# Spreading a kernel's weight loads over a phase of small products, and moving some vector work behind the results that free TensorE

## The chip, the cores and the metric

The kernel runs on one core of a Trainium2 chip. The metric is device time of one execution in microseconds; the values given are the median of several runs and the runs' own spread. The profile is one further execution, recorded by the hardware profiler. Its times count from the start of the profiled span.

## The reference

Two blocks follow each other. The first is a delta-rule attention with a state per head, the second a two-layer network with a PReLU between the layers.

```python
# q, k, v: (4, 8, 768, 48); beta: (4, 8, 768)
for t in range(S):
    y[:, :, t] = einsum('bhd,bhde->bhe', q[:, :, t], state)
    v_old = einsum('bhde,bhd->bhe', state, k_n[:, :, t])      # k_n: k by its norm
    state = state + beta_t * einsum('bhd,bhe->bhde', k_n[:, :, t], v[:, :, t] - v_old)
# x: y as (3072 tokens, 384); w_in: (384, 2048); w_out: (2048, 384)
h = x @ w_in
g = maximum(h, 0) + alpha * minimum(h, 0)
out = g @ w_out
```

The weights w_in and w_out arrive as float64, 6.3 MB each; everything else that matters here is float32.

## The kernel before, in words

The sequence of 768 tokens is cut into 12 chunks of 64, and the batch of 4 into 2 pairs. A step is one chunk of one pair with all its heads, so there are 24 steps. Within a step the recurrence over the 64 tokens is replaced by products of small matrices: the keys are transposed (`flip`, L383), their Gram matrix is made (`grams`, L435) and weighted, a triangular matrix is inverted, and the state is applied and renewed (`through_state` L774, `solve` L799, `outputs` L812, `next_state` L828). The triangular inverses of four steps at a time are made together. Its blocks of 32 are turned so that VectorE eliminates them column by column (`eliminate`: two instructions for each column, L527 and L533, between transposes, L500). For the first four steps only blocks of 16 are eliminated, and the halves are joined by small products on TensorE (`cross`, L604, L614 and L621, "the cross products").

The order on every engine is written out by hand. All instructions of an engine stay in program order, and `weave` mixes several generators by shares: each gives its pieces evenly over the length of the mixture, some starting at a given fraction of it. SP issues nearly all DMAs, in program order; each waits on SP for its buffer to be free, and what stands behind it waits too.

The loads of a step are `load_early` (keys, tile ke, 2 DMAs), `load_q` (qp, 2), `load_v` (v_raw, 2) and `load_late` (keys in another layout, kl, 4). Step n takes ke three steps ahead.

The weights are converted from float64 to float32 in the kernel. `weights` cuts a matrix into pieces, fetches each as raw 32-bit words into a staging place (L209), and converts it by two ScalarE instructions (`begin`, L225 and L226) and two VectorE instructions (`finish`, L235 and L240). w_in has 12 pieces of 512 KB. Their staging places are six parts of the w_out tile, which is not needed yet: pieces 0 to 5 are fetched at once, and each later piece when the one that had its place is converted. w_out has 16 pieces of 384 KB. Their places are three in a tile of their own, `space_out`, and four in the upper half of w_out.

The part that the change touches begins with `first_chunk`, which takes steps 0 and 1 through the attention. `second_pair` then does steps 2 and 3, mixed by `alongside` with the first layer of chunk 0 (`ffn_in(0)`, L942: eight pairs of 128 columns of w_in, in two banks by turns) and with the conversions. A bank of `ffn_in` is freed when ScalarE has made its negative part (L952) and VectorE the PReLU from it (L954). Two weaves follow: `ffn_in(1)` with conversions of w_out and 15 of the elimination's pieces (`SOON`), and `ffn_out(0)` (L985) with the remaining ones. Later, in the steps JOINED = 6 to 23, a step has three stretches; `PIECES_OF` gives the share of elimination pieces for each, and `weight_sums` (L929) makes differences of quarters of w_out for a faster form of the second layer.

Of the kernel before, what the change touches and what calls it, by code (L numbers as in the profile page):

```python
# [43 lines left out]
def kernel(  # L44
# [94 lines left out]
    def load_early(n, *queues):  # L139
        if n < N:  # L140
            fetch(k, n, early(n)[:, :, 0:D], *queues)
# [29 lines left out]
    SPACES = 3  # L171
# [7 lines left out]

    ahead = [0]  # L180

    def weights(pieces, stages, ids, done):

        count = len(pieces)
        fetched, begun = [], []

        def words(i):
            w = stages[ids[i]]
            dst, src = pieces[i]
            shape = list(dst.shape)
            n = shape[1] * (shape[2] if len(shape) > 2 else 1)
            w = w[:, 0 : 2 * n]  # L200
            if len(shape) > 2:
                return w.rearrange("p (f e) -> p f e", f=shape[1]), n
            return w, n

        def fetch(n):
            while len(fetched) < min(n, count):
                i = len(fetched)
                assert ids[i] not in ids[len(done) : i]
                nc.sync.dma_start(out=words(i)[0], in_=pieces[i][1].bitcast(U32))  # L209
                fetched.append(i)  # L210

        def flat(x):
            return x.rearrange("p f d -> p (f d)") if len(x.shape) > 2 else x

        def halves(i):
            w = flat(words(i)[0]).rearrange("p (e w) -> p e w", w=2)
            return w[:, :, 0], w[:, :, 1], flat(pieces[i][0])

        def begin(n):
            while len(begun) < min(n, count):  # L220
                i = len(begun)
                assert i < len(fetched)
                lo, hi, dst = halves(i)

                nc.scalar.activation(dst.bitcast(U32), lo, ACT.Copy, scale=2.0**-29)  # L225
                nc.scalar.activation(  # L226
                    lo.bitcast(FP32), hi.bitcast(FP32), ACT.Prelu, scale=2.0**-112, alpha=-(2.0**32)
                )
                begun.append(i)

        def finish():
            for i in range(count):
                begin(min(i + 2, max(ahead[0], i + 1)))
                lo, _, dst = halves(i)
                nc.vector.tensor_scalar(  # L235
                    out=lo, in0=lo, scalar1=3, scalar2=None, op0=ALU.logical_shift_left
                )
                yield

                nc.vector.tensor_tensor(  # L240
                    out=dst.bitcast(U32), in0=lo, in1=dst.bitcast(U32), op=ALU.add
                )
                done.append(i)
                n = len(fetched)
                while n < count and ids[n] not in ids[i + 1 : n]:
                    n += 1
                    fetch(n)
                yield

        return fetch, begin, finish()  # L250
# [94 lines left out]
    def squared(n):  # L345
        ksq[n] = work.tile([128, H, D], FP32, name="ksq", bufs=2)
        nc.scalar.square(ksq[n], early(n)[:, :, 0:D])  # L347

    def norms(n):
        stats[n] = work.tile([128, H], FP32, name="norm", bufs=EARLY + 3)  # L350
        nc.vector.tensor_reduce(out=stats[n], in_=ksq.pop(n), axis=AXX, op=ALU.add)  # L351
# [67 lines left out]
    def now(pieces):  # L419
        for x in pieces:  # L420
            x()
# [40 lines left out]
    NJ = 4  # L462
# [965 lines left out]
    def first_chunk(mask, convert):  # L1428

        both = (0, 1)  # L1430
        ahead[0] = n_in

        waits, pause = iter([0.5] * 2), []
        middle = cross(
            0, slice(0, 2 * H), edge, half_way, lambda: pause and busy(next(waits, 0), pause[0])
        )
        next(middle)
        pause.append(ps_one())
        busy(1, pause[0])
        begin_in(6)  # L1440
        for i in both:
            scale_v(i)
            mask(i)
        convert(2)
        next(middle)
        busy(1.25)
        place(0, (0,))
        place(1, (0,), True)
        for i in both:
            place(i, (1,), True)  # L1450
            now(between_1(i))
        keys = flipped(NJ, ps_ffn())
        convert(2)
        for i in both:
            place(i, (2,))
            now(between_2(i))
        now(keys)
        for i in both:
            now(through_state(i))
            now(solve(i))  # L1460
        now(flipped(NJ + 1, ps_ffn()))
        for i in both:
            now(outputs(i))
        convert(4)
        for i in both:
            to_ffn(i, ps_ffn())
        now(flipped(NJ + 2, ps_one()))
        for i in both:
            squared(NJ + i)
        load_early(NJ + NKE)  # L1470
        ahead[0] = FT * DM
        convert(4)
        for i in both:
            norms(NJ + i)

    def statics(first, last):
        if first > 0:
# [21 lines left out]
    ]  # L1499
    n = 2 * W_IN_P  # L1500
    n_in = FT * DM // n
    ids = [i % n_in for i in range(len(pieces))]
    fetch_in, begin_in, conv_in = weights(
        pieces, [space[:, i * n : (i + 1) * n] for i in range(n_in)], ids, in_done
    )
    PARTS_IN = 2 * len(pieces)

    pieces = [(w_out[:, f], moe_w_out[f * 128 : (f + 1) * 128]) for f in range(FT)]
# [19 lines left out]
    fetch_in(n_in)  # L1528
    squares(0)
    betas()  # L1530
    for _ in statics(0, NJ - 1):
        pass
    nc.scalar.copy(inside, ones)
# [22 lines left out]
            pass  # L1556

    first_chunk(mask, convert)
    fetch_out(SPACES)
    assert n + 22 == PARTS_IN + 10  # L1560

    first_in = ffn_in(0)
# [6 lines left out]
    def second_pair():  # L1569

        n, m, x = 2, 3, NJ
        both = (n, m)
        halves = [cross(0, slice(i * H, i * H + H), edge, half_way) for i in both]
        for i in range(2):
            now(next_state(i))
            load_late(i + 2)
            load_v(i + 3)
            alongside(2, 1)
        for h in halves:
            next(h)  # L1580
        flips(x + 3, n)
        load_early(x + 1 + NKE)
        load_q(n + 2)
        squares(x + 2)
        now(weigh(x))
        alongside(5, 2)
        next(halves[0])
        flips(N, m)
        load_early(x + 2 + NKE)
        load_q(n + 3)  # L1590
        now(weigh(x + 1))
        place(n, (0,))
        alongside(4, 2)
        next(halves[1])
        now(weigh(x + 2))
        place(m, (0,))
        alongside(2, 1)
        now(grams(x))
        squares(x + 3)
        alongside(2, 1)  # L1600
        for i in both:
            now(between_1(i))
        now(grams(x + 1))
        load_early(x + 3 + NKE)
        alongside(7, 3, (chain(*(placing(i, (1, 2, 3)) for i in both)), 6))
        for i in both:
            now(between_2(i))
        now(grams(x + 2))
        for i in both:
            scale_v(i)  # L1610
        now(weigh(x + 3))
        alongside(5, 3)
        y = ps_big()
        pieces = []
        for i in range(2):
            pieces += through_state(n + i, None, y[:, :, i * G * D : (i + 1) * G * D])
        now(pieces)
        alongside(5, 3)
        y = ps_big()
        pieces = []  # L1620
        for i in range(2):
            pieces += solve(n + i, y[:, :, i * G * D : (i + 1) * G * D])
        now(pieces)
        now(grams(x + 3))
        alongside(5, 2)
        y = ps_big()
        pieces = []
        for i in range(2):
            pieces += outputs(n + i, y[:, :, i * G * D : (i + 1) * G * D])
        now(pieces)  # L1630
        alongside(5, 2, (part(blocks, PIECES), PIECES))
        for i in both:
            to_ffn(i)
        for i in both:
            alongside(2 * (m - i), 0)
            now(next_state(i))
            load_late(i + 2)
            load_v(i + 3)
        alongside(IN_PARTS - 46, 1, (part(blocks, 1), 1))

    blocks, BEGUN, SOON, LAST = eliminate(1), PIECES + 1, 15, 6
    second_pair()
    fetch_out(len(stages))
    weave(
# [3 lines left out]
    for i in range(2):  # L1648
# [1 line left out]
    load_q(NJ + 2)  # L1650
    n = WHOLE + PIECES - BEGUN - SOON
    weave(
        (conv_out, OUT_PARTS // 2), (part(blocks, n), n),
        (statics(FIRST + NJ, EARLY + 3), 2 * (EARLY + 4 - FIRST - NJ) + 1),
        (ffn_out(0, True), OUT_PARTS),
    )
# [61 lines left out]
    for n in range(NJ, JOINED):  # L1718
# [7 lines left out]
    assert next(late, None) is None  # L1726
    PIECES_OF = {
        JOINED: (3, WHOLE - 2 * PIECES - 6 - 2 * share - 3, 2 * PIECES),
        JOINED + 1: (1, 4, 7), JOINED + 2: (4, 4, 5),
    }  # L1730
    TURNS = [(3, 3, 4), (3, 3, 4), (4, 4, 4), (0, 5, 6)]
    FILL = {JOINED: (8, 12, 12), JOINED + 1: (10, 12, 10), JOINED + 2: (8, 10, 12)}
# [2 lines left out]
    for n in range(JOINED, N):  # L1735
# [4 lines left out]
        if n == JOINED:  # L1740
            place(n + 1, (0,))
            extra[1] = [(weight_sums(1, 0, 3), 3)]
            extra[2] = [(weight_sums(0, 3, 4), 1)]
        elif n == JOINED + 1:
            extra[0] = [(weight_sums(1, 3, 4), 1), (placing(n + 1, (1, 2, 3)), PLACING)]

        later = burst_a(n)
        stretch(fill[0], blocks, share[0], later, *extra[0], *put_off)
# [63 lines left out]
```

## Time and profile before

| | |
|---|---|
| median of 3 runs | 664.44 us (662.76 to 664.89) |
| profiled execution | 665.1 us, of it the span 663.3 us |
| TensorE busy | 642.9 us, 97% of the span |
| VectorE busy | 491.9 us, 74% |
| ScalarE busy | 263.9 us, 40% |
| GpSimd busy | 92.9 us, 14% |
| moved by DMA | 37.72 MB in 110,963 packets |
| granted TensorE clock | 1.00 |

The profile names engines PE (TensorE), DVE (VectorE), ACT (ScalarE), POOL (GpSimd) and SP. PEld is the loading of weights into TensorE, which overlaps its products. A busy share is the mean over the whole span, and the stages differ: the transfers lie mostly in the first sixth, and VectorE is near its limit in some stretches and half idle in others. In a list of waits each row gives who waited, for whom, the total, how often, and the longest. In a timeline each row gives start and duration, the operation and its shapes, and in brackets the idle time before it with what ended it.

### The profile page before, as it was taken

To read this page: it belongs to the slowest core of one execution; us is meant where nothing else is said; L and a number is where in the kernel's file an instruction comes from. 1 tells how busy PE (TensorE), PEld (TensorE's weight loads), DVE (VectorE), ACT (ScalarE), POOL (GpSimd) and SP (SyncE) were. 2 spreads that over 40 slices of the span, in tenths; PEclk is the share of its full clock that TensorE was granted. 3 is DMA by queue.
4 is the path that set the end of the run, shared out by engine and by line. 5 is a ranking of instruction groups with operands and counts; after the bars stand their busy time and mean duration, and the time that the engine had idled before them with its cause. 6 is when DMAs were issued, how large, how long until landed. Compare 5 with 4: busy or idle time off the path is not lost.

```text
span 663.3 us, 22123 instructions
## 1 busy us (share of the span) xinstructions
PE 642.9 (97%) x9545; PEld 567.3 (86%) x9545; DVE 491.9 (74%) x1180; ACT 263.9 (40%) x621; POOL 92.9 (14%) x201
## 2 busy tenths in 40 slices
PE   5997999999999999999999999999999999999997
PEld 4576888556788988998998998988999999999997
DVE  4964799967999869748859748858868658568383
ACT  4945766334454252243343243232135245042140
POOL 6000210100000100001000000000035044053250
PEclk9999999999999999999999999999999999999999
DMA  8848645301432122122112111112111210100000
GB/s 119 249 119 223 157 108 141 84 25 35 73 67 49 26 53 46 26 49 50 26 38 37 27 38 37 26 38 38 26 41 35 41 32 4 31 9 2 24 1 25
DMA packets 110963, 37.72 MB, mean 57 GB/s; under 512 B 104161, under 2 KB 107249, under 8 KB 110865
## 3 DMA queue, kind: packets, MB, share of 16 engines
q1 hardware_dynamic: 109088, 35.81, 24.5%
q8 instruction: 75, 1.23, 0.7%
q10 hardware_dynamic: 1776, 0.49, 0.4%
q14 instruction: 24, 0.19, 0.1%
HBM read 31.56 MB, written 4.72 MB: 55 GB/s over the span
## 4 chain that ended last, share of the span: by engine, by line
PE 79%; DVE 12%; DMA 3%; ACT 3%; issue 1%; ACTq 0%; SPq 0%; DVEq 0%
PE p_ffn L1007 17%; PE p_ffn L942 16%; PE p_more L1259 8%; PE p_ffn L985 5%; PE p_more L1175 4%; PE p_ffn L1165 3%; PE p_ffn L1259 3%; PE p_ffn L1170 2%; PE p_pair L383 2%; PE p_pair L685 2%; DMA ke<-in_k_dram 2%; PE p_pair L774 2%; PE p_pair L799 2%; PE p_pair L1403 2%; PE p_pair L812 2%; PE p_pair L435 2%
## 5 line engine op out<-in xcount | busy, mean ns | idle before, releaser
L942 PE MATMUL p_ffn<-xt,w_in 128*128 128x256 f32 x768 | 176.1, 383 | 2.0 <-DVE act L954 2.0
L942 PEld LDWEIGHTS p_ffn<-xt,w_in 128*128 128x128 f32 x768 | 142.4, 190 | 22.6 <-issue 2.9
L954 DVE SCALAR_TENSOR_TENSOR act<-act,al_t,p_ffn 128x256 f32<-128x256 f32 x112 | 48.7, 476 | 29.1 <-ACT act L952 29.1
L952 ACT ACTIVATE act<-p_ffn 128x512 f32<-128x512 f32 x56 | 33.3, 595 | 82.4 <-PE p_ffn L942 82.2
L533 DVE TENSOR_TENSOR block<-block,prod 128x30 f32<-128x30 f32 (+9 forms) x150 | 49.9, 332 | 5.1
L1199 POOL TENSOR_TENSOR k_t<-k_t 128x128 f32<-128x128 f32 (+1 forms) x48 | 29.2, 609 | 167.4 <-ACT k_t L1194 164.9
L527 DVE TENSOR_TENSOR prod<-block 128x30 f32<-128x30 f32 (+9 forms) x150 | 48.8, 326 | 1.3
L1007 PE MATMUL p_ffn<-w_out,act 128*128 128x192 f32 x288 | 49.6, 328 | 0.0
L372 POOL TENSOR_TENSOR beta_t<-beta_t,rec 128x8 f32<-128x8 f32 x24 | 6.5, 270 | 291.7 <-DVE rec L370 275.2
L1007 PEld LDWEIGHTS p_ffn<-w_out,act 128*128 128x128 f32 x288 | 46.5, 190 | 0.3
L853 ACT COPY xt<-p_pair 128x384 f32<-128x384 f32 x22 | 10.4, 478 | 90.7 <-PE p_pair L851 76.9
L1199 POOL TENSOR_TENSOR block<-block 128x128 f32<-128x128 f32 (+1 forms) x48 | 27.6, 575 | 17.3 <-ACT block L1194 14.8
L1165 PE MATMUL p_ffn<-xt,w_in 128*128 128x256 f32 x96 | 28.7, 381 | 0.5 <-DVE o_sb L1027 0.5
L784 DVE TENSOR_TENSOR r<-v_raw,p_pair 64x192 f32<-64x192 f32 (+1 forms) x66 | 23.3, 353 | 2.3 <-PE p_pair L774 1.2
L351 DVE TENSOR_REDUCE norm<-ksq 128x8 f32<-128x384 f32 x24 | 12.9, 546 | 16.2 <-ACT ksq L347 16.2
L803 DVE TENSOR_TENSOR u<-p_pair,wgt 128x384 f32<-128x384 f32 x24 | 13.2, 555 | 15.4 <-PE p_pair L685 14.3
L697 ACT COPY inv<-p_pair 32x256 f32<-32x256 f32 x40 | 14.4, 361 | 25.3 <-DVE u L803 24.5
L1213 DVE SCALAR_TENSOR_TENSOR act<-block,al_t,act 128x256 f32<-128x256 f32 x32 | 19.7, 657 | 5.3 <-ACT block L1209 5.2
L985 PE MATMUL p_ffn<-w_out,act 128*128 128x384 f32 x64 | 21.8, 491 | 1.1 <-DVE more L954 1.1
L1027 DVE TENSOR_TENSOR o_sb<-u,p_ffn 128x192 f32<-128x192 f32 x24 | 7.9, 351 | 19.6 <-PE p_ffn L1007 19.5
L763 ACT COPY y<-p_pair 128x384 f32<-128x384 f32 x22 | 10.4, 478 | 30.2 <-PE p_pair L759 28.6
L1259 PE MATMUL p_more<-w_out,act 128*128 128x192 f32 x128 | 21.8, 329 | 0.0
(226 smaller groups left out, 1410.9 us busy)
## 6 DMA issues: line engine op xcount, KB each, us to landing
w_out<-in_moe_w_in_dram SPq DMA_DIRECT2D x12, 512.0 KB, 5.7
qp<-in_q_dram SPq DMA_DIRECT2D x48, 96.0 KB, 3.0
v_raw<-in_v_dram SPq DMA_DIRECT2D x48, 96.0 KB, 2.9
kl<-in_k_dram SPq DMA_DIRECT2D x96, 48.0 KB, 2.5
out_dram<-o_sb SPq DMA_DIRECT2D x92, 48.0 KB, 1.6
space_out<-in_moe_w_out_dram SPq DMA_DIRECT2D x11, 384.0 KB, 3.3
ke<-in_k_dram SPq DMA_DIRECT2D x43, 96.0 KB, 3.2
w_out<-in_moe_w_out_dram SPq DMA_DIRECT2D x5, 384.0 KB, 4.3
```

Source lines behind the costliest of these rows:

```text
L527: nc.vector.tensor_tensor(out=prod, in0=r[:, 0:j, j : j + 1].to_broadcast([128, j, n]), in1=r[:, j : j + 1, j + 1 : HB].to_broadcast([128, ...
L533: nc.vector.tensor_tensor(out=r[:, 0:j, j + 1 : HB], in0=r[:, 0:j, j + 1 : HB], in1=prod, op=ALU.add)
L784: nc.vector.tensor_tensor(out=r[to, a], in0=v_in[to, a], in1=p[own, a, :, 0:D], op=ALU.subtract)
L942: nc.tensor.matmul(p_h[:, i], w_in[:, t, (f + i) * 128 : (f + i + 1) * 128], xt[:, t], start=(t == 0), stop=(t == KT - 1),)
L952: nc.scalar.activation(g, p_h, ACT.Relu, scale=-1.0)
L954: nc.vector.scalar_tensor_tensor(out=g[:, i], in0=g[:, i], scalar=al_t[:, f + i : f + i + 1], in1=p_h[:, i], op0=ALU.mult, op1=ALU.add,)
L985: nc.tensor.matmul(p_o[u], gs[f // 2][:, f % 2, u * 128 : (u + 1) * 128], w_out[:, f], start=(f == 0), stop=(f == FT - 1),)
L1007: nc.tensor.matmul(p, x(i), w(i), start=(i == 0), stop=(i == FP - 1))
L1165: nc.tensor.matmul(p[:, f * 256 : f * 256 + 256], w(2, f), xt[:, 2], start=True, stop=False)
L1175: nc.tensor.matmul(q[:, j], a, b, start=True, stop=True)
L1199: nc.gpsimd.tensor_tensor(out=dst, in0=a, in1=b, op=ALU.add)
L1259: nc.tensor.matmul(p, x(i), w(i), start=(i == 0), stop=(i == FP - 1))
```

## The change

Five things change.

- Eight pieces of w_in are fetched in the first burst; pieces 6 and 7 are staged in `space_out`, in which two pieces of w_out are staged later. Pieces 8 to 11 take the places of pieces 2, 3, 0 and 1. Only piece 8 is still fetched by the conversion that frees its place (`limit`).
- In `second_pair`, pieces 9 to 11, the first three pieces of w_out and the steps' loads are issued by hand, in alternation, from the first `next_state` to the second Gram matrix. The first piece of w_out comes after the second step of the cross products.
- In `first_chunk`, the squares of the keys of steps 4 and 5, the load of step 7's keys and the first norm move ahead of `through_state`.
- The first weave takes 12 pieces of the elimination instead of 15; five of the rest are given from 0.55 of the second weave on.
- In step JOINED + 1 no piece of the elimination stands in the first stretch (before: one), and the last difference of w_out's quarters is put at 0.6 of it; step JOINED + 2 takes five pieces instead of four in its second.

```diff
-    def weights(pieces, stages, ids, done):
+    def weights(pieces, stages, ids, done, limit=None):
...
-                while n < count and ids[n] not in ids[i + 1 : n]:
+                while n < min(count, limit or count) and ids[n] not in ids[i + 1 : n]:
...
         now(keys)
         for i in both:
+            squared(NJ + i)
+        load_early(NJ + NKE)
+        norms(NJ)
+        for i in both:
             now(through_state(i))
             now(solve(i))
...
         now(flipped(NJ + 2, ps_one()))
-        for i in both:
-            squared(NJ + i)
-        load_early(NJ + NKE)
         ahead[0] = FT * DM
         convert(4)
-        for i in both:
-            norms(NJ + i)
+        norms(NJ + 1)
...
-    ids = [i % n_in for i in range(len(pieces))]
-    fetch_in, begin_in, conv_in = weights(
-        pieces, [space[:, i * n : (i + 1) * n] for i in range(n_in)], ids, in_done
-    )
+    stages = [space[:, i * n : (i + 1) * n] for i in range(n_in)]
+    spare_words = space_out.rearrange("p s e -> p (s e)")
+    stages += [spare_words[:, i * n : (i + 1) * n] for i in range(2)]
+    ids = [*range(n_in + 2), 2, 3, 0, 1]
+    fetch_in, begin_in, conv_in = weights(pieces, stages, ids, in_done, n_in + 3)
...
     fetch_in(n_in)
     squares(0)
     betas()
+    fetch_in(n_in + 2)
...
     first_chunk(mask, convert)
-    fetch_out(SPACES)
...
-        for i in range(2):
-            now(next_state(i))
-            load_late(i + 2)
-            load_v(i + 3)
-            alongside(2, 1)
+        now(next_state(0))
+        load_late(2)
+        alongside(2, 1)
+        now(next_state(1))
+        fetch_in(n_in + 4)
+        load_v(3)
+        alongside(2, 1)
         for h in halves:
             next(h)
+        load_late(3)
+        fetch_in(n_in + 5)
         flips(x + 3, n)
-        load_early(x + 1 + NKE)
-        load_q(n + 2)
         squares(x + 2)
         now(weigh(x))
         alongside(5, 2)
         next(halves[0])
+        fetch_in(n_in + 6)
+        load_early(x + 1 + NKE)
         flips(N, m)
-        load_early(x + 2 + NKE)
-        load_q(n + 3)
         now(weigh(x + 1))
         place(n, (0,))
         alongside(4, 2)
         next(halves[1])
+        fetch_out(1)
+        load_q(n + 2)
+        load_early(x + 2 + NKE)
         now(weigh(x + 2))
         place(m, (0,))
         alongside(2, 1)
         now(grams(x))
         squares(x + 3)
+        fetch_out(2)
+        load_q(n + 3)
         alongside(2, 1)
         for i in both:
             now(between_1(i))
         now(grams(x + 1))
+        fetch_out(3)
+        load_v(4)
         load_early(x + 3 + NKE)
...
-    blocks, BEGUN, SOON, LAST = eliminate(1), PIECES + 1, 15, 6
+    blocks, BEGUN, SOON, LAST = eliminate(1), PIECES + 1, 12, 6
...
-        (conv_out, OUT_PARTS // 2), (part(blocks, n), n),
+        (conv_out, OUT_PARTS // 2), (part(blocks, n - 5), n - 5), (part(blocks, 5), 5, 0.55),
...
-        JOINED + 1: (1, 4, 7), JOINED + 2: (4, 4, 5),
+        JOINED + 1: (0, 4, 7), JOINED + 2: (4, 5, 5),
...
-            extra[0] = [(weight_sums(1, 3, 4), 1), (placing(n + 1, (1, 2, 3)), PLACING)]
+            extra[0] = [(weight_sums(1, 3, 4), 1, 0.6), (placing(n + 1, (1, 2, 3)), PLACING)]
```

## The prediction

> **What bounds the kernel now.** TensorE. I read the page's busy table first, then TensorE's waits, then its timeline at the waits, then what DMA and VectorE do there.
>
> ```profile
> PE   642.9 (97%) x9545; PEld 567.3 (86%) x9545; DVE 491.9 (74%) x1180; ACT 263.9 (40%) x621; POOL 92.9 (14%) x201
> ```
>
> TensorE is idle for 663.3 - 642.9 = 20.4 us in all. The change leaves every TensorE instruction and their order as they are (the two instruction lists are equal), so it can only win idle time. The waits of TensorE (total, times, longest, in us) say where that is:
>
> ```profile
> PE p_ffn L942 <- DVE act L954: 2.0, 2, 1.5
> PE p_pair L621 <- issue: 1.8, 1, 1.8
> PE p_pair L604 <- issue: 1.6, 1, 1.6
> PE p_ffn L985 <- DVE more L954: 1.1, 1, 1.1
> PE p_pair L799 <- issue: 0.7, 1, 0.7
> PE p_pair L720 <- issue: 0.5, 1, 0.5
> PE p_pair L383 <- DMA ke<-in_k_dram: 0.4, 1, 0.4
> ```
>
> Apart from the first 20 us, which the change doesn't touch, nearly all of it stands here. "issue" means that no semaphore explains the wait. The timeline of TensorE gives the places (start, us, count, idle before):
>
> ```profile
> 39.21 1.17 PE L720 MATMUL p_pair<-diag,right 64*64 64x32 f32 x33 [0.55 <-issue]
> 44.09 0.81 PE L799 MATMUL p_pair<-v_raw,inv 64*64 64x48 f32 x39 [0.72 <-issue]
> 53.74 0.71 PE L604 MATMUL p_pair<-turned,sums 32*32 32x16 f32 x63 [1.61 <-issue]
> 54.85 0.62 PE L383 MATMUL p_pair<-ident,ke 128*112 128x128 f32 x4 [0.40 <-DMA ke<-in_k_dram]
> 60.58 0.60 PE L621 MATMUL p_pair<-inverse,act 32*32 32x16 f32 x49 [1.77 <-issue]
> 120.82 7.98 PE L985 MATMUL p_ffn<-w_out,act 128*128 128x384 f32 x24 [1.13 <-DVE more L954]
> 209.34 2.83 PE L942 MATMUL p_ffn<-xt,w_in 128*128 128x256 f32 x12 [1.51 <-DVE act L954]
> ```
>
> The four "issue" waits break off in the middle of a group. Counting TensorE's records (weight loads and matmuls) up to each gives 1217, 1473, 1985 and 2241 instructions: each is a multiple of 256 plus 193. The DMA table has a queue that moves the instructions themselves:
>
> ```profile
> q8 instruction: 75, 1.23, 0.7%
> ```
>
> 75 packets of 16 KB for 19,090 TensorE instructions is one packet for about 256. So TensorE stands at a block boundary, waiting for its next block. The packed trace has the blocks that end the four waits: they land at 37.8, 42.8, 52.0 and 59.1, and TensorE goes on 1.3 to 1.8 us after each. From crossing one boundary to the start of the next block's packet it takes 1.1 to 1.5 us where few large packets are about, but 2.6 us (crossing at 39.2), 2.9 (48.2) and 4.5 (53.7) where they are. Dense small products use up 256 instructions in 3.7 to 4.9 us there, so 1.4 + 1.0 (the packet) + 1.4 = 3.8 us just holds and anything above stalls. What DMA does then, by windows (the last three numbers of a row are the granted clock, DMA's busy share and its GB/s; the first pair after the length is TensorE's):
>
> ```profile
> 36.00:39.00 3.00, 2.44 (x41) 1.66 (x35) 2.81 (x8) 0.51 (x1) 0.00 (x0) 1.00 0.76 206
> 40.00:43.00 3.00, 3.00 (x99) 2.78 (x98) 0.42 (x1) 1.65 (x4) 0.00 (x0) 1.00 0.57 171
> 47.00:60.00 13.00, 9.80 (x275) 7.81 (x272) 6.94 (x16) 8.94 (x20) 0.47 (x2) 1.00 0.95 283
> 60.00:66.00 6.00, 5.42 (x183) 4.50 (x186) 3.48 (x11) 3.31 (x9) 0.47 (x2) 1.00 0.54 76
> ```
>
> From 47 to 60 us four pieces of w_in and three of w_out stand in SP's queue nearly back to back; TensorE works 9.8 of 13 us.
>
> [...] A 512 KB piece is 8 records of 4 KB on each of 16 engines at about 165 ns, 1.3 us; [...] I treat the fetch as standing behind what was issued before it.
>
> **The change part by part.**
>
> (1) Pieces 6 and 7 of w_in come in the first burst. Now that burst is 16.0 to 24.5 us for six pieces; eight take 2 x 1.3 = 2.6 us more. The steps' loads behind it (ke, kl, v, q: 16 DMAs on SP) slip by about that, plus 2 x 0.5 us of issue: ke of step 4 lands near 29 us and is flipped at 40.3, kl for step 1 near 34 and is read at 49.7, so 9 us or more of cover. The block fetched at 24.0 comes at 26.6, usable near 29; needed at 30.8. Cost 0. In return the bursts of pieces 6 and 7 at 36 and 40 us are gone. For the fetch behind the stall at 39.21 there remain the q loads: start 35.1 + 1.4, landed 37.5, usable 38.9 instead of 39.2: **-0.3**. For 44.09 nothing large is left: usable near 42.6, before it is needed; but L799 then waits briefly for VectorE's L740 (ends 43.5): **-0.6**.
>
> (2) ksq of steps 4 and 5 (2 x 0.52 us on ScalarE) and one norm reduction (0.55 us on VectorE) move ahead of through_state. ScalarE is idle from 42.1 to 45.5 and VectorE from 43.5 to 44.5: covered, except that the reduction may hold the first L803 by up to 0.4 us, behind which TensorE has L383 (0.6 us). 0. The early load of ke for step 7 goes from 49.2 to about 43, so the wait of 0.40 for it goes: **-0.4**.
>
> (3) Pieces 8 to 11, the loads and three w_out pieces alternate on SP. Piece 8 is issued when piece 2 is converted (46 us), piece 9 after kl (4 x 0.65 us), then v, kl, then 10 and 11 together. A fetch that crosses near 47.5 then finds 1.3 us ahead of it instead of three pieces: stall 1.78 to about 0.4, **-1.4**. That at 58.8 finds one piece: 1.77 to 0.1, **-1.7**. The next fetch now lies near 56, where pieces 10 and 11 come together (2.6 us); it had no reserve before (landed 62.8, used at 64.2). Usable 1 to 1.8 us late, or not at all if the pieces come after it: **+0.9**.
>
> On SP the new wait is that of w_out piece 0 for the conversion of piece 7 (VectorE, 60.4 now, about 57 then). Behind it stand q, ke, two w_out pieces, v, ke, w_out 3 to 6. The first needed of these is w_out 0 on ScalarE, L225 at 75.9 now; it would land near 60. Cover over 10 us. POOL's stream is unchanged.
>
> (4) Twelve elimination steps instead of fifteen in the first weave: 3 x (0.40 + 0.41 us, L527 and L533 at their widest) leave VectorE's queue ahead of the last L954, which ends at 120.6 and holds L985. VectorE is without a pause from 76 to 137 us, so it all counts: 2.4 us earlier, limited by ScalarE's L952 (ends 118.4). The wait of 1.13 goes nearly whole: **-1.0**. The steps come back in the second weave, whose later part (130 to 150 us) has VectorE at 72% and 58%: 0.
>
> (5) One transpose piece (L500) and L929 no longer stand ahead of the L954 that frees TensorE at 209.34. The chain there is VectorE's alone:
>
> ```profile
> 206.41 0.86 DVE w_out L929
> 207.28 0.60 DVE sums L896
> 207.88 0.58 DVE block L500
> 208.47 0.74 DVE act L954 x2
> ```
>
> 0.86 + 0.58 = 1.44 us; L952 for it ended at 206.7. The later L929 falls into 2.7 us of matmuls. **-1.4**.
>
> Sum: -0.3 - 0.6 - 0.4 - 1.4 - 1.7 + 0.9 - 1.0 - 1.4 = **-5.9 us**. The profiled execution took 665.1 us (span 663.3), so 659.2; the median of the runs is 0.66 us lower, which makes 658.5. I round towards no gain, **659.0**, since fetches weren't measured under the new mix. Bounds: all seven waits of the timeline gone is -7.7 (656.7); the fetch terms at half (-1.7) and (4), (5) whole gives 660.3.
>
> **Rivals.** (a) The stalls move to other blocks: the fetch is slow whenever SP streams anything, and several of the blocks from 45 to 69 us were within 1.5 us of stalling. For it: 2.4 us of latency at 43.1, with DMA nearly idle (though 1.5 if counted from TensorE's restart). Then only ke, (4) and (5) remain, -2.8: 661.6. (b) No change: VectorE, 98% busy from 80 to 120, takes back what TensorE wins, or the orders are reshuffled without effect: 664.4. Against it: VectorE waits for TensorE before 76 us and so starts earlier by as much. (c) Slower: SP's in-order wait of w_out 0 for piece 7 makes L225 late; ScalarE is in order, so L952 and TensorE stand behind it. It decides once w_out 0 lands after about 72 us, 12 us later than I place it, and has to eat 5.9 us of gains first; at 80 us it gives 667. Nothing in the profile points to such a delay.
>
> **How the numbers follow.** My forecast 0.70, (a) 0.17, (b) 0.08, (c) 0.05. About 0.3% (2 us) can be told from no change. (a) lies just beyond that line, so nearly all its chance counts as faster: faster 0.86, same 0.09, slower 0.05. The range runs from all waits gone, 656.7, to (a) with some loss, 662.4.
>
> **What would show it.** Right: TensorE's list of waits without "issue" above 1 us between 36 and 66 us, no wait for ke, L985 and L942 starting at most 0.3 us after their releaser; DMA share between 47 and 60 us spread to 0.6 or 0.7; q8 packets starting within 2.7 us of the crossing. Wrong: new "issue" waits at 193 above other multiples of 256 that add up to the old 4.65 us, ScalarE's L225 waiting for w_out or space_out, or the L954 waits merely moving on by a group.

## The result, and the profile after

Over 20 runs each the median went from 664.18 to 661.84 us: ratio 0.9965, 95% interval 0.9942 to 0.9988. A second comparison, the last but one of the experiments below, gave 0.9930 (0.9903 to 0.9958). So the change helps by 2.3 us in the first and 4.7 in the second, where 5.4 were forecast from the median; the second interval (2.8 to 6.5 us) takes in the forecast, the first (0.8 to 3.9) doesn't. Medians and ranges hold all runs; the ratios leave out the runs that are more than 1.5% above the fastest of their kernel. The profiled execution of the changed kernel took 664.18 us (span 662.5), 0.9 below that of the kernel before; it is one of its slower ones.

First TensorE's waits in the profile after (who waited for whom: total us, times, longest), without those of the first 20 us and two that were the same before (L1165, 0.5, and L774, 0.2):

```profile
PE p_pair L621 <- issue: 4.5, 2, 3.6
PE p_ffn L942 <- DVE act L954: 0.5, 1, 0.5
PE p_pair L720 <- ACT diag L653: 0.4, 1, 0.4
```

All seven waits of the prediction's timeline are gone or shorter in this profile: no "issue" at L720, L799 and L604, none for ke, none of 1 us or more for L954. The 0.5 us for L954 was there before, at 255 us; the wait of L720 for ScalarE (L653) grew from 0.2 to 0.4. In their place stand two "issue" waits in the second step of the cross products. TensorE's timeline after (start, us, idle before):

```profile
55.31 0.28 PE L621 MATMUL p_pair<-inverse,act 32*32 32x16 f32 x12
56.55 0.60 PE L621 MATMUL p_pair<-inverse,act 32*32 32x16 f32 x50 [0.95 <-issue]
...
63.92 0.62 PE L621 MATMUL p_pair<-inverse,act 32*32 32x16 f32 x31 [3.57 <-issue]
64.47 2.08 PE L942 MATMUL p_ffn<-xt,w_in 128*128 128x256 f32 x4
```

They break off at instructions 2241 and 2497, again 193 above a multiple of 256. (The count takes in TensorE's semaphore instructions, which the prediction's "weight loads and matmuls" leaves out: 25 and 27 of them and one DRAIN stand ahead of these two places, and 16 to 24 ahead of the four places before.) In the six fetches before these a block's packet starts 1.0 to 3.2 us after TensorE has crossed the boundary ahead of it. The block that ends the long wait follows the crossing at 56.55; its packet starts at 61.0 and lands at 62.2. SP's timeline shows what was issued just before:

```profile
55.63 1.07 SPq L209 DMA_DIRECT2D w_out<-in_moe_w_in_dram  x2
56.80 1.29 SPq L137 DMA_DIRECT2D ke<-in_k_dram  x2
58.65 0.34 SPq L209 DMA_DIRECT2D space_out<-in_moe_w_out_dram  x1
```

The two DMAs of the first row are pieces 10 and 11 of w_in. Their packets run from 56.9 to 61.1 us. Then, in the last row of the timeline above, four products L942 take 2.08 us; in the kernel before such a group took 1.13. The windows of the profile after say why (after the stretch: total, TensorE, weight loads, VectorE, ScalarE, GpSimd; then granted clock, DMA share, GB/s; the share sums the times of all packets and so can exceed 1):

```profile
60.00:62.00 2.00, 0.35 (x39) 0.28 (x30) 1.11 (x3) 1.16 (x4) 0.00 (x0) 0.99 1.20 241
62.00:64.00 2.00, 0.08 (x6) 0.08 (x9) 0.36 (x1) 0.00 (x0) 0.00 (x0) 0.50 1.13 196
64.00:66.00 2.00, 2.00 (x35) 1.60 (x34) 1.26 (x5) 0.80 (x2) 0.27 (x1) 0.50 1.10 137
66.00:68.00 2.00, 2.00 (x35) 1.41 (x34) 0.33 (x1) 1.34 (x3) 0.21 (x1) 0.50 0.72 216
68.00:70.00 2.00, 2.00 (x32) 1.49 (x31) 1.52 (x4) 0.00 (x0) 1.16 (x2) 0.80 0.90 173
```

TensorE runs at half clock from about 62 to 69 us. The 256 instructions after the long wait took 6.93 us (63.92 to 70.85); the same ones took 4.77 before. So some 2.2 us more were lost after the wait was over.

The balance of this execution: waits gone -7.69 (the seven), new ones +4.52, half clock +2.2, together -1.0; the span fell by 0.9.

The clock is not a matter of this one execution. Over the 20 runs of the changed kernel, time and mean granted clock go together (correlation -0.91; a straight line through them gives 4.9 us for 0.01 of clock). The 8 runs at 0.999 or above (called full clock below; what such a mean leaves out is told at the changed kernel's second profile) have a median of 659.5 us, the other 12 one of 664.3. The kernel before has such runs too: 43 of its 57 on the first chip of the experiments are below 0.999.

### The profile page after: what moved, and what is told of

It is laid out like the page before. It is cut to its first block, busy times and chain, and to the rows that moved or that the text cites. A ratio compares the mean times of both kernels' runs of the same rounds, so it can differ in the third digit from the quotient of the medians.

```text
span 662.5 us, 22123 instructions
## 1 busy us (share of the span) xinstructions
PE 644.9 (97%) x9545; PEld 569.0 (86%) x9545; DVE 490.3 (74%) x1180; ACT 264.4 (40%) x621; POOL 93.7 (14%) x201
## 3 DMA queue, kind: packets, MB, share of 16 engines
q8 instruction: 75, 1.23, 0.8%
## 4 chain that ended last, share of the span: by engine, by line
PE 91%; DVE 4%; ACT 2%; issue 1%; DMA 1%; ACTq 0%; DVEq 0%
PE p_ffn L942 24%; PE p_ffn L1007 17%; PE p_more L1259 8%; PE p_ffn L985 5%; PE p_more L1175 4%; PE p_ffn L1165 3%; PE p_ffn L1259 3%; PE p_pair L383 3%; PE p_pair L774 2%; PE p_ffn L1170 2%; PE p_pair L685 2%; PE p_pair L435 2%; PE p_pair L799 2%; PE p_pair L812 2%; PE p_pair L1403 2%; PE p_pair L759 1%
## 5 line engine op out<-in xcount | busy, mean ns | idle before, releaser
L942 PE MATMUL p_ffn<-xt,w_in 128*128 128x256 f32 x768 | 177.6, 385 | 0.7 <-DVE act L954 0.5
L942 PEld LDWEIGHTS p_ffn<-xt,w_in 128*128 128x128 f32 x768 | 143.4, 191 | 21.5 <-issue 1.5
L954 DVE SCALAR_TENSOR_TENSOR act<-act,al_t,p_ffn 128x256 f32<-128x256 f32 x112 | 48.6, 475 | 28.0 <-ACT act L952 28.0
L1165 PE MATMUL p_ffn<-xt,w_in 128*128 128x256 f32 x96 | 28.7, 381 | 0.5 <-DVE o_sb L1027 0.5
L1194 ACT COPY k_t<-p_more 128x512 f32<-128x512 f32 x16 | 9.4, 587 | 31.4 <-PE p_more L1175 26.7
```

What stands on the lines that cost most here:

```text
L942: nc.tensor.matmul(p_h[:, i], w_in[:, t, (f + i) * 128 : (f + i + 1) * 128], xt[:, t], start=(t == 0), stop=(t == KT - 1),)
L954: nc.vector.scalar_tensor_tensor(out=g[:, i], in0=g[:, i], scalar=al_t[:, f + i : f + i + 1], in1=p_h[:, i], op0=ALU.mult, op1=ALU.add,)
L1165: nc.tensor.matmul(p[:, f * 256 : f * 256 + 256], w(2, f), xt[:, 2], start=True, stop=False)
```

## The experiments

Theory 1: a block of TensorE's instructions (a packet of 16 KB, one for about 256) is fetched behind the pieces that SP has issued. Two pieces together hold it for longer than the reserve. TensorE then idles, and in this stage idling halves its clock (1.00 to 0.50 in the profile after). Theory 2: the slow clock comes by chance, or the fetches are held up by the steps' small loads; the pieces have nothing to do with it. Theory 3: only the bytes in the stage count, not where the pieces stand. The diffs show the lines that matter, with ... between them. Kernels that are compared below by their medians ran on the same chip unless it is said otherwise.

**The two halves of the change apart.** First the kernel before with VectorE's orders alone:

```diff
+    blocks, BEGUN, SOON, LAST = eliminate(1), PIECES + 1, 12, 6
...
+        (conv_out, OUT_PARTS // 2), (part(blocks, n - 5), n - 5), (part(blocks, 5), 5, 0.55),
...
+        JOINED + 1: (0, 4, 7), JOINED + 2: (4, 5, 5),
...
+            extra[0] = [(weight_sums(1, 3, 4), 1, 0.6), (placing(n + 1, (1, 2, 3)), PLACING)]
```

> The kernel before with only the two edits to VectorE's order (12 elimination pieces in the first weave with five of the rest from 0.55 of the second; L929 and one transpose behind the L954 of step JOINED + 1). Both theories: the waits of TensorE at L985 (1.13 us) and L942 (1.51 us) go, the four issue waits between 39 and 61 us stay as they were, clock 1.00: about 661.8 us, 2.4 below the kernel before. If it gains less than 1 us, VectorE's order was not what these waits were worth.

Measured: 661.76 us against 664.44 of the kernel before, ratio 0.9956 (0.9934 to 0.9978), so -2.9 us. Both waits for L954 are gone from its profile. The issue waits didn't stay "as they were": in this execution they were 0.97 (L604), 0.68 and 0.28 (L621), and the wait for ke was 1.09. The stalls of 0.55 and 0.72 us at 39 and 44 us are missing here as well, with the loads of before. The same loads meet the fetches differently from one execution to the next.

Then the changed kernel with these four lines undone, so that the loads alone are changed:

> The changed kernel with VectorE's two orders put back to those of before, so that only the loads and the early squares are changed. Theory 1 (the fetch of TensorE's next block stands behind pieces 10 and 11, the stall grows past 3 us, and TensorE's clock halves after it): a long issue wait between 55 and 65 us in most runs, those with the clock below 0.997 take 664 to 667 us, those at 1.00 some 661 to 662; median about 664. Theory 2 (the slow clock comes by chance and has nothing to do with the loads): no difference in clock from the kernel before; median 661 to 662.

Measured: 664.06 us, ratio 1.0001 (0.9975 to 1.0027). Its timeline has the two VectorE waits again:

```profile
119.03 7.98 PE L985 MATMUL p_ffn<-w_out,act 128*128 128x384 f32 x24 [0.92 <-DVE more L954]
...
207.54 2.83 PE L942 MATMUL p_ffn<-xt,w_in 128*128 128x256 f32 x12 [1.48 <-DVE act L954]
```

The long wait is not in this profile, which ran at a clock of 1.00: its issue waits add up to 2.9 us, with 0.68 and 0.29 (L621) where the changed kernel had 0.95 and 3.57, and 1.21 at the next boundary, at 67.41 us.

So on this chip VectorE's orders are worth all that the change brings, and moving the loads nothing on the whole; on the chip where the change gave 4.7 us the halves were not taken apart. The loads are not without effect, though: the 8 of 22 runs at full clock have a median of 662.1 (the kernel before: 663.05, 14 of 57), the others 667.5 (664.9). By these medians the loads' new places make good executions a little better and bad ones worse.

**Without pieces 10 and 11.**

```diff
-                nc.sync.dma_start(out=words(i)[0], in_=pieces[i][1].bitcast(U32))
+                if limit is None or i < 10:
+                    nc.sync.dma_start(out=words(i)[0], in_=pieces[i][1].bitcast(U32))
```

> The changed kernel without the two DMAs of pieces 10 and 11 of w_in (their places are converted with what they hold, so the first layer uses wrong weights there; all else is the same). Theory 1: the wait of 3.57 us at L621 falls below 0.7 us, no run's clock goes below 0.998, and the time is 657 to 659 us. Theory 2: the clock still drops in about half of the runs, and the median stays near 661.8; a fetch held up by the steps' small loads would leave the wait of 3 us or more.

Measured: 657.65 us, ratio 0.9875 (0.9841 to 0.9910). All six runs lie between 655.6 and 658.9 and at a clock of 0.999 or above. The kernel leaves out these two transfers and so works with wrong weights. All of TensorE's issue waits after 30 us in its timeline (its lines are one higher, L721 is L720):

```profile
39.44 1.17 PE L721 MATMUL p_pair<-diag,right 64*64 64x32 f32 x33 [0.56 <-issue]
...
65.53 0.30 PE L721 MATMUL p_pair<-diag,right 64*64 64x32 f32 x4 [0.24 <-issue]
```

The steps' small loads and the w_out pieces are all still there. What speaks against theory 2 are the runs: 6 of 6 are at full clock and at 658.9 us or below; of the changed kernel's 20 runs 8 are at full clock and one is as fast. The missing long wait alone would not, since of the three profiles with both pieces together at this place one has it (3.57 us) and two don't. Theory 3 is left as it was, because 1 MB went as well.

**Where the pieces go instead.** Ten at once, with 10 and 11 together near 42 us:

```diff
+    spare_words = more.rearrange("p i s e -> p (i s e)").bitcast(U32)
+    stages += [spare_words[:, i * n : (i + 1) * n] for i in range(2)]
+    ids = [*range(n_in + 4), 0, 1]
...
+    fetch_in(n_in + 4)                        # the first burst
...
+        fetch_in(n_in + 6)                    # in first_chunk, before between_2
-        fetch_in(n_in + 4)                    # and the three in second_pair
```

> The changed kernel with ten pieces of w_in in the first burst (pieces 8 and 9 in the tile more, free until the first layer of chunk 1) and 10 and 11 issued after the q loads near 41 us, while DMA is idle; no piece of w_in is left for the stage from 45 to 65 us. Theory 1: the issue waits between 50 and 65 us go below 0.7 us, one of up to 1.2 us may come near 47, the clock stays at 1.00 in all runs: 658 to 659.5 us. Theory 2: median about 662 with the same spread of clocks as the changed kernel.

Measured: 661.56 us, ratio 0.9953 (0.9934 to 0.9973): no better than the changed kernel, and 16 of 22 runs below a clock of 0.999, against my number. In the profile the same thing stands in another place. The two pieces are issued at 41.6 us; the block fetched after the crossing at 42.5 has its packet at 46.3 and comes 1.77 us late:

```profile
48.81 0.87 PE L828 MATMUL p_pair<-u,kl 64*64 64x48 f32 x23 [1.77 <-issue]
```

It is the only issue wait from 30 to 135 us. Where no piece stood any more, at the three fetches from 54 to 63 us, the block landed 1.4 to 2.6 us before it was needed. This is not all reserve, as I took it to be in later expectations: after a stall TensorE went on 1.3 to 1.8 us after the landing.

**Piece 11 moved away from piece 10.**

```diff
-        fetch_in(n_in + 6)
         load_early(x + 1 + NKE)
...
+        fetch_in(n_in + 6)
         fetch_out(1)
```

> The changed kernel with piece 11 of w_in moved from directly behind piece 10 to directly ahead of the first w_out piece; all else as it is. Theory 1 (it is the pieces standing together ahead of one fetch): the fetch crossing near 56 us finds one piece of w_in, its stall falls from 3.6 us to below 1.5, the clock rarely drops: 659 to 660.5 us. Theory 3 (what counts is the number of bytes in the stage from 50 to 65 us, wherever they stand): the stall moves to the fetch that crosses near 60 us with the same 3 us or more, 661.5 to 662.5.

Measured: 660.59 us, ratio to the kernel before on this chip 0.9930 (0.9903 to 0.9957). The median lies just above where theory 1 put it, but the changed kernel, run again on this chip later, has the same ratio. So this doesn't tell the theories apart. In its profile (664.7 us) the waits of more than 1 us are 1.22 and 1.49, at 56.7 and 68.8; the clock is halved from 58.1 and from 68.3 us.

**All twelve at once,** with nothing of w_in left for later:

```diff
+    for x, first in ((act, 1024), (more, 0)):
+        spare_words = x.rearrange("p i s e -> p (i s e)").bitcast(U32)[:, first:]
+        stages += [spare_words[:, i * n : (i + 1) * n] for i in range(2)]
+    ids = [*range(n_in + 6)]
...
+    fetch_in(n_in + 6)
```

> The changed kernel with all twelve pieces of w_in in the first burst (8 and 9 in parts of the tile act, 10 and 11 in the tile more, all free until converted); the steps' loads behind it come 5 us later. Theory 1: no issue wait above 0.8 us anywhere from 36 to 66 us, clock 1.00 in nearly all runs, 656.5 to 658.5 us and a spread below 4 us. Against it stands that the loads of steps 4 to 6 are late (ke landing after 40 us would hold TensorE at L383): then 659 or more with a wait for ke or kl in the list.

Measured: 663.61 us, ratio 0.9962 (0.9937 to 0.9987). Neither ke nor kl is late. The burst now lasts into the fetch that crosses at 30 us, which is 1.55 us late at 35.98. There is no other issue wait, yet 13 of 15 runs are below full clock, and in the profile it is halved from 38 to 51 us. By a straight line through its runs it would take about 659 us at full clock. So runs at low clock, with their stalls, cost some 4.5 us, three times the stall in the profile.

With the first three w_out pieces later as well:

```diff
-        fetch_out(1)
...
-        fetch_out(2)
```

> As the kernel with twelve pieces at once, and the first three w_out pieces together behind the second Gram matrix (near 66 us) instead of one by one from 58 us. Theory 1: the fetch that crosses near 60 us meets no large piece any more; what is left of issue waits between 58 and 66 us falls below 0.3 us, and the time is 0 to 0.7 us below that of the kernel with twelve at once. If ScalarE's L225 then waits for space_out near 75 us, it is slower instead.

Measured: 664.62 us, ratio 0.9967 (0.9942 to 0.9991). Nothing is gained; the stall at 36 us stays (1.50). There was hardly anything to win: the list of waits of the twelve at once has no other issue wait.

**More bytes where the kernel before has them.**

```diff
                 nc.sync.dma_start(out=words(i)[0], in_=pieces[i][1].bitcast(U32))
+                if count == 12 and i >= 10:
+                    spare_words = more.rearrange("p i s e -> p (i s e)").bitcast(U32)
+                    nc.sync.dma_start(
+                        out=spare_words[:, (i - 10) * 1024 : (i - 9) * 1024],
+                        in_=pieces[i][1].bitcast(U32),
+                    )
```

> The kernel before, with pieces 10 and 11 of w_in each fetched a second time, into a tile that is free then (1 MB more in the stage from 50 to 60 us, no other change). Theory 1: the fetch behind the wait of 1.77 us near 59 us comes about 2.5 us later, the wait grows to 3.5 us or more, TensorE's clock halves for some us after it: 668 to 671 us, clock 0.99 or below. Theory 2 (chance): the wait may grow, but the clock behaves as in the kernel before: at most 667.

Measured: 668.88 us, ratio 1.0039 (1.0016 to 1.0063), none of 19 runs at full clock, median clock 0.992. The time is that of theory 1 and the clock nearly, but the one long wait didn't come. In the profiled execution there are 1.29, 1.23 (for ke) and 1.09 us, and the clock is halved twice.

**Two better places.** Eleven at once, and ten at once with each of the last two alone; the third row is the changed kernel again, on the same chip:

```diff
# eleven
+    fetch_in(n_in + 5)            # the first burst
...
+        fetch_in(n_in + 6)        # piece 11, behind load_late(3)
# ten, two apart
+    fetch_in(n_in + 4)            # the first burst
...
         fetch_in(n_in + 5)        # piece 10, behind load_late(3), as in the changed kernel
...
+        fetch_in(n_in + 6)        # piece 11, ahead of fetch_out(1)
```

> Eleven pieces of w_in in the first burst (8 and 9 in parts of act, 10 in more), piece 11 alone behind the second kl load near 54 us, all else as in the changed kernel. Twelve at once lost 1.55 us at the fetch that crosses near 30 us, behind the end of the burst, and then ran at half clock; one piece fewer ends the burst 1.3 us earlier. Theory 1: no issue wait above 0.7 us, clock mostly 1.00, 657.5 to 660 us. If a stall at 36 us stays above 1 us, 661 or more with a wide spread.

> Ten pieces of w_in in the first burst, piece 10 alone behind the second kl load and piece 11 alone ahead of the first w_out piece, all else as in the changed kernel. Ten at once left 1.7 us of reserve at the fetch of 30 us and 2.6 and 1.4 us at those of 54 and 59 us when no piece stood there. Theory 1: each single piece costs about 1.3 us of a reserve that is there: no issue wait above 0.5 us, 657 to 659.5 us, spread below 5 us. If a single piece costs as much as two, 661 to 662.

> The changed kernel once more, on the same chip as the two with more pieces at once. 661.8 us as before. Theory 1: its profile has issue waits of 1 us or more near 56 or 64 us again; if their sum is below 2 us and the clock is 1.00, this execution takes 659 to 660 us; if one is above 3 us, or the clock falls, 662 or more.

| | median, range (us) | ratio to before | runs below 0.993 of clock |
|---|---|---|---|
| eleven at once | 663.48 (657.8 to 667.2) | 0.9957 (0.9936 to 0.9978) | 17 of 22 |
| ten, two apart | 659.87 (657.6 to 661.6) | 0.9918 (0.9883 to 0.9953) | 0 of 8 |
| changed kernel again | 661.54 (657.3 to 668.7) | 0.9930 (0.9903 to 0.9958) | 4 of 19 |

Eleven at once stalls for 1.43 us at 36 us, the case that its expectation named last. Ten with the two apart has no issue wait above 0.62 us and the narrowest spread of those that load everything, though over 8 runs only. It is faster than the kernel before; its interval overlaps with that of the changed kernel, so against that one only the median (1.7 us lower) and the spread speak. It doesn't decide between theories 1 and 3: it sets the two pieces apart, and it also has 1 MB less in the stage after 45 us. Theory 3 stays open.

The changed kernel's own profile this time has issue waits of 0.40, 1.52 and 0.87 us and 659.26 us. Its clock was low too (0.995), but from 15.8 to 22.7 us, and my "if the clock falls, 662 or more" was wrong. This shows a limit of the figure. The record of the clock begins with its first rise (at 25.3 us in the profile before, at 24.4 in the first one after), and what lies before counts as full. Yet eight transposes L383 at 16.41 us took 1.95 us in the profile before and 1.96 in this one; four of them take 0.60 at 47.5 us and took 1.10 at 9.8. So TensorE ran at half clock in both, and only this profile counts it. (The kernel with VectorE's orders alone has the same: 0.995, from 17.6 to 24.4 us, 659.95 us.) A mean of 0.995 can thus come from this early stretch alone; one below 0.993 can't come from 6.8 us at half clock.

**Idling without a transfer.** The stage after 30 us has filler products, which keep TensorE at work while it would wait. In the kernel with the two pieces apart I took one group out; no DMA changes.

```diff
         next(middle)
-        busy(1.25)
         place(0, (0,))
```

> The kernel with ten pieces at once and the last two apart, without the filler products busy(1.25) in first_chunk (products into an unused bank, whose results nobody reads). All DMAs stay as they are; TensorE then stands idle for about 1.5 us from 36 us on, waiting for VectorE and ScalarE as it would anyway, where the kernel with eleven pieces stood for 1.43 us. Theory 1 (the halved clock comes from TensorE's idling in this stage, whatever it waits for): the clock is halved from about 39 to 52 us in the profile and below 0.993 in most runs; median 663 to 665 us. Rival (the halved clock comes with the transfers, or by chance): clocks and time as with the filler, 659 to 660.5 us.

Measured: 663.15 us (ratio 0.9987, 0.9965 to 1.0009, on another chip), and all 22 runs have a clock of 0.992 or below; with the filler it was 0 of 8. The chips differ, but the kernel before is that low in 10 of 27 runs on this one and in 20 of 42 on the other. Its timeline and windows, the columns as above:

```profile
34.66 1.10 PE L621 MATMUL p_pair<-inverse,act 32*32 32x16 f32 x93 [1.26 <-issue]
37.26 3.62 PE L720 MATMUL p_pair<-diag,right 64*64 64x32 f32 x64 [1.50 <-ACT diag L653]
```

```profile
35.00:40.00 5.00, 3.50 (x126) 3.39 (x116) 3.07 (x8) 0.88 (x2) 0.00 (x0) 0.59 0.47 85
40.00:45.00 5.00, 5.00 (x82) 4.59 (x79) 0.42 (x1) 2.48 (x6) 0.00 (x0) 0.50 0.46 88
45.00:50.00 5.00, 5.00 (x143) 4.49 (x142) 4.05 (x9) 1.06 (x2) 0.00 (x0) 0.54 0.13 24
```

The same stretch with the filler:

```profile
35.00:40.00 5.00, 4.46 (x162) 3.62 (x150) 3.07 (x8) 0.88 (x2) 0.00 (x0) 1.00 0.48 84
40.00:45.00 5.00, 4.83 (x172) 4.30 (x176) 2.73 (x7) 2.93 (x7) 0.00 (x0) 1.00 0.58 103
```

DMA's share is the same or lower without the filler, TensorE gets through 82 records from 40 to 45 us instead of 172, and the clock goes from 1.00 to 0.50. So in this stage the low clock goes with TensorE's idling and not with the DMAs, which are the same: without the filler it came in every run. The profile doesn't show that this one wait is enough. The clock falls at 35.91 us, only 0.15 us into the wait of 1.50; what lies just ahead of the fall is the fetch wait of 1.26.

## Why the prediction was wrong

The mechanism held in its kind: stalls at block boundaries (0.95 and 3.57 us, at instructions 2241 and 2497), in some of them behind w_in's pieces, and two waits for VectorE. That a fetch stands behind what was issued before it was my estimate, from a piece's 1.3 us and packets that started up to 4.5 us after the crossing; no profile shows what held a packet back. What failed is the last term of step (3) and one that was not in the sum.

- (1) The stalls of 0.55 and 0.72 us are gone whole in the profile; I had -0.3 and -0.6. That is not shown to be the change's work, since the kernel with VectorE's orders alone doesn't have them either, and the one without pieces 10 and 11 has 0.56 us at the first place. Two more pieces in the first burst cost nothing, as said. Eleven or twelve in all do, as the stalls at 36 us showed.
- (2) The wait for ke is gone, as said.
- (3) The stall of 1.61 us at L604 (1.78 in the prediction's sum) is gone (forecast: its greater part); that of 1.77 fell to 0.95 instead of 0.1. The step that failed is "**+0.9**" for the next fetch, with nothing for the ones behind it. In the profiled execution it was 3.57. I had both pieces flowing from the crossing on. In fact they were issued at 55.6 and 56.3, data came only from 56.9 us, and the packet came when both were nearly through, at 61.0. That is 4.45 us after TensorE went on, where my bound of 1.8 us on the stall allowed 2.7. In the other two profiles with the same loads this stall was 0.29 us or absent, but others came behind it: from this boundary on they add up to 1.5 us with the loads alone and to 2.4 in the second profile of the changed kernel. So the term of 0.9 measured 1.5 to 3.6 us; without pieces 10 and 11 it was 0.24. Why its size and place vary between executions was not found.
- Not in the sum: half clock after a stall. In the profiled execution it took 2.2 us; the other two profiles have none in this stage. On the whole the fetch terms and ke, -3.5 by my sum, came to 0.0 (the kernel with the loads alone: interval -1.7 to +1.8 us).
- (4) and (5): -2.4 by my sum; both waits went, and the kernel with these edits alone measures -2.9 (-4.4 to -1.5). VectorE took nothing back. (It is not without a pause up to 137 us, as the prediction has it: from 130 us on it was busy 82% of the time.)
- Of the rivals, (a) came nearest to the time, 661.6, and partly to the cause: the stalls did move to other blocks. In the long one the pieces had moved there; but (a) is not refuted: in the kernel without pieces 10 and 11 the packet of one block still started 2.9 us after the crossing (at 60.2 us). (c) didn't occur, and its premise was off: w_out 0 lies over piece 6 alone, and SP issued it at 58.65.

At full clock the changed kernel's median was 659.5 us, near the forecast of 659.0, but that is no confirmation: the forecast started from the median of all runs, and the kernel before has 663.05 us at full clock, so a like comparison gives some 3.5 us. In these traces the clock falls to 0.50, and the length of a wait alone doesn't tell when: the kernel with twelve pieces at once waited 1.55 us up to 35.98 and its clock fell at 37.7 us, while no fall followed the wait of 1.77 us up to 60.58 in the profile of the kernel before. In the profiles before and after, the changes of the clock lie whole multiples of 3.41 us apart (187 in the one; 11, 2 and 174 in the other; the last fall comes 0.3 us behind the span in both), on a grid that stands differently in each (25.31 us is on the one, 24.42 on the other). In the experiments' profiles the stretches at half clock last one, two, four or five times 3.41 us. Counted back from the fall, the wait up to 35.98 lay whole in one such stretch (34.29 to 37.70 us, TensorE busy 54%); the one up to 60.58 lay across two (81% and 67%). Nine of the ten falls after 30 us follow a stretch with TensorE busy for 33 to 76%, the tenth one of 91%; but four stretches between 55% and 67% in the profile before, and one of 72% in the profile after, had no fall behind them. So the grid can be part of why executions differ; what decides was not shown.

## What to carry to other kernels

Where TensorE runs many small products, count its instructions, semaphores included, up to an "issue" wait: if the counts share a remainder by 256 (193 here), look for the large transfers that were issued around the time the block was asked for, and try at most one piece of 0.5 MB for each block's fetch. That is where the best median came from here, over 8 runs; one piece for each fetch wasn't enough in the kernel with piece 11 moved. Read the granted clock by window beside each wait of more than a microsecond, and price the stretch after it at half clock as well (3.4 to 17.1 us here, where the clock fell). Here the burst could be lengthened from six to ten pieces; at eleven it reached a fetch without reserve, and TensorE waited 1.43 us. Profile the same kernel more than once: three profiles of the same loads had 3.57, 1.21 and 1.52 us as their longest issue wait.

## What the runs showed of the hardware

- Without one group of filler products, in whose place TensorE waited 1.50 us, the ratio to the kernel before was 0.9987 instead of 0.9918, and the clock was 0.992 or below in all of 22 runs instead of none of 8 (on different chips). A straight line through the runs of a kernel gives 4.6 to 5.4 us for 0.01 of mean clock in ten of sixteen sets, 2.2 to 5.9 us in the other six; the kernel without pieces 10 and 11, whose clocks are all 0.999 or 1.000, is left out.
- In the profiles before and after, the changes of the granted clock lie whole multiples of 3.41 us apart (187 before; 11, 2 and 174 after). In the eight profiles in which it fell after 30 us it stayed at half for 3.4 to 17.1 us at a time.
- A mean clock of 1.00 doesn't tell of the first 24 us: eight transposes took 1.95 us at 16.4 us in a profile with a mean of 1.00, and 1.96 us in one with 0.995, where the record has half clock at this time.
- The fetch of a 16 KB block, whose packet takes about 1 us, started up to 4.5 us after TensorE had gone on, with 1 MB of pieces issued around that time.
